# Scratch writes of row-maximum reductions sent to two bfloat16 SBUF tiles, and one output buffer instead of two, in a four-layer attention and MLP kernel

## The chip, the cores and the metric

The kernel runs on one core of one Trainium2 chip. The metric is the device time of one execution in microseconds (us); the median of three runs of the kernel before is 1586.9 us (1585.45 to 1589.74). Engines are named as in the profile: PE (matrix multiply), PEld (its weight loads), DVE (vector), ACT (scalar), POOL (GpSimd), SP (the engine that only issues DMAs here). PSUM is the memory that PE writes its products to, SBUF the working memory.

## What is computed

Two kinds of layer, A and B, follow each other twice on a sequence of 2048 rows of 640 numbers. A is attention with 32 heads of 20 dimensions, in which a row sees itself and the 255 rows before it; B is an MLP of width 1536 with a squared ReLU.

```python
def _A_ref(x, wqkv, wo):
    ...
    scores = jnp.einsum("bhqd,bhkd->bhqk", q, k) * (Dh ** -0.5)
    mask = (idx[:, None] - idx[None, :] >= 0) & (idx[:, None] - idx[None, :] < W)
    scores = jnp.where(mask[None, None], scores, -1e9)
    p = _softmax(scores, axis=-1)
    o = jnp.einsum("bhqk,bhkd->bhqd", p, v)
    return (lambda x, *d: x.transpose(*d))(o, 0, 2, 1, 3).reshape(B, S, D) @ wo
...
x = x + _A_ref(_layernorm(x, axis=-1), A_wqkv, A_wo)
x = x + _B_ref(_layernorm(x, axis=-1), B_w1, B_b1, B_w2, B_b2)
x = x + _A_ref(_layernorm(x, axis=-1), A_wqkv, A_wo)
x = x + _B_ref(_layernorm(x, axis=-1), B_w1, B_b1, B_w2, B_b2)
```

## The kernel before

**Units and quads.** The sequence is cut into 8 blocks of 256 rows; with two passes through A and B that makes 16 units, numbered 0 to 15. In a unit the 32 heads are taken four at a time: 8 quads a unit, 128 in all. Weights and activations are split into a high and a low float16 part, so each dense product is three matmuls per piece of 128 (`mm3`, L327), 256 or 320 columns wide. The dense work of a unit is: query and key rows (`stage_qk`, in the profile `acc<-yT,wq_s`), value rows (`stage_v`, `acc<-wq_s,yT`), the product with wo (`stage_o`, `acc<-wo_s,od`), and the two MLP products (`stage_f`, `acc<-y,w_s` and `acc<-w_s,hh`). In the first units some of these operands lie in borrowed tiles, so that `acc<-kt,wq_s` and `acc<-wq_s,kt` are also query, key and value work, of unit 1.

**One quad.** It has three parts on PE.
- `max_quad` (L653, L668 in the first unit of a pass) computes the raw scores into six PSUM banks, `bb6` (three for each half of the heads). DVE then makes eight reductions, `reduce` (L633): each reads 320 columns of scores from PSUM and a bfloat16 mask from SBUF (`maskq`; 128 or 256 columns and `maskw` in units 0 and 8), adds the two, writes the sum back over the scores and leaves the row maximum in `mx`. On the chip that is two instructions, the reduction and a read of the accumulator. After each two quads (a group) the maxima are turned and written into spare rows of the queries by SP DMAs (`rows_out`, L689, `qt<-mT` or `qt<-mt`): in units 0 and 1 through a PE transpose (`max_out`, L721), later through a transposing DMA (`max_cross`, L709).
- `exp_quad` (L757, L765) computes the scores again, transposed and with the maximum already subtracted, into the same six banks. ACT takes the exponentials (L779, six a quad, four in units 0 and 8) into `pt` tiles, and POOL zeroes what the window leaves out (L794, L798).
- `pv_quad` (L828) multiplies by the values. ACT copies the product to `ot` (L840), one tile for two quads, and after the second SP writes the tile to memory with four DMAs (L845). When the eight quads of a unit are written, `load_o` reads the sums and products back (L871, L872), DVE and ACT divide and split them (L904 to L914), and `stage_o` can start.

So the banks pass around a ring: scores, reductions, transposed scores, exponentials, next scores. The maxima run three quads ahead of the exponentials (`LEAD`).

**What sets the order.** The program fixes the order of every engine itself (`manual_schedule`). A planner runs while the program is built: `post` enters a job with an engine, a cost in ns, what it depends on and a priority; `pump` puts a job into the program when the planner's clock reaches it; `flow` (unit 0) and `together` (the others) ask, before each part of a quad, whether the jobs it needs are over on the planner's clock, and put pieces of dense work on PE until they are. The planned cost of a job thus sets how much dense work stands between two parts of a quad. A wait that the planner doesn't know, such as a buffer that is not yet free, is added by the framework as a semaphore wait and moves nothing. The wait of the copy into `ot` is of that kind: the planner lets `ot<-pv` depend on the product alone.

The functions that the change touches:

## Time and profile before

| | |
|---|---|
| median of three runs | 1586.9 us |
| the profiled execution | 1589.08 us, its span 1587.4 us |
| busy over the span | PE 98%, PEld 74%, DVE 62%, ACT 46%, POOL 38% |
| granted TensorE clock | 0.997 |
| costliest DVE group | the reductions L633, 409.3 us in 896 of 320 columns |
| DMA | 160.44 MB, mean 101 GB/s |

A row of a timeline gives start, duration, engine, source line, operation, output<-input, shape and count; what stands in brackets is how long the engine was idle before and what released it. Matmuls overlap in the pipeline, so the mean duration of one (around 300 ns) is not its cost; the distance from start to start is. Of the other 1.7 us of the profiled execution the span shows nothing.

### The profile page before, as it was taken

What the parts mean: (1) busy time and instruction counts of PE and PEld (TensorE: products, weight loads), DVE (VectorE), ACT (ScalarE), POOL (GpSimd) and SP (SyncE); (2) the same over time, 40 slices, a digit from 0 to 9 for tenths busy, and PEclk for the clock granted to TensorE, in tenths of its full rate; (3) what the DMA queues carried; (4) which work ended last, traced back from release to release, by engine and by line L of the source; (5) the groups of instructions that cost most, each with busy time, mean ns of one, the idle gap of its engine ahead of it and who ended that gap; (6) DMA issues with size and microseconds to landing.
All of it is one profiled execution on the core that took longest, in us unless ns stands there. A gap on an engine that the chain in (4) does not pass through costs nothing. (4 is left out here: it accounts for less than half of the span.)

```text
span 1587.4 us, 52465 instructions
## 1 busy us (share of the span) xinstructions
PE 1556.4 (98%) x21534; PEld 1167.0 (74%) x21534; DVE 984.3 (62%) x3253; ACT 733.9 (46%) x1593; POOL 600.2 (38%) x1291
## 2 busy tenths in 40 slices
PE   8989999999999999999999999999999999999999
PEld 7666767777777777778777777777777777776767
DVE  8777665656756656665566656557665666756431
ACT  4555445444453444535343453544545345454612
POOL 1234434234252433525323352442535235253612
PEclk9999999999999999999999999999999999999999
DMA  9864344362533525354352534434343353431120
GB/s 265 208 181 105 77 110 87 101 128 52 121 87 106 108 61 133 70 125 86 97 132 59 119 87 116 98 88 110 71 123 83 98 117 69 107 87 58 29 67 18
DMA packets 243209, 160.44 MB, mean 101 GB/s; under 512 B 91160, under 2 KB 226712, under 8 KB 242968
## 3 DMA queue, kind: packets, MB, share of 16 engines
q1 hardware_dynamic: 236600, 147.58, 39.3%
q10 hardware_dynamic: 6368, 9.50, 2.1%
q8 instruction: 169, 2.77, 0.8%
q14 instruction: 72, 0.59, 0.1%
HBM read 84.68 MB, written 52.95 MB: 87 GB/s over the span
## 5 line engine op out<-in xcount | busy, mean ns | idle before, releaser
L779 ACT ACTIVATE pt<-bb 128x512 f32<-128x512 f32 (+1 forms) x736 | 375.9, 601 | 226.4 <-PE bb L757 203.2
L633 DVE CUSTOM_DVE_ANT_0 bb<-bb,maskq 128x320 f32<-128x320 f32 x896 | 409.3, 523 | 89.7 <-PE bb L653 76.1
L794 POOL TENSOR_SCALAR_AFFINE_SELECT pt<-pt 128x256 f32<-128x256 f32 x448 | 188.6, 423 | 564.1 <-ACT pt L779 550.9
L327 PE MATMUL acc<-y,w_s 128*128 128x256 f16 x2880 | 330.0, 274 | 2.5 <-ACT y L377 1.4
L327 PE MATMUL acc<-w_s,hh 128*128 128x320 f16 x2304 | 326.0, 299 | 0.0
L327 PEld LDWEIGHTS <-w_s 128*128 128x128 f16 x2880 | 277.3, 98 | 55.2 <-issue 17.9
L327 PEld LDWEIGHTS <-hh 128*128 128x128 f16 x2304 | 220.6, 98 | 98.1 <-issue 11.5
L327 PEld LDWEIGHTS <-wq_s 128*128 128x128 f16 x2400 | 229.5, 98 | 46.5 <-issue 13.9
L327 PE MATMUL acc<-yT,wq_s 128*128 128x256 f16 x2250 | 258.7, 273 | 2.7 <-DVE qd L510 1.3
L798 POOL TENSOR_SCALAR_AFFINE_SELECT pt<-pt 128x256 f32<-128x256 f32 x512 | 213.6, 439 | 90.5 <-ACT pt L779 88.8
L1013 DVE TENSOR_TENSOR hh<-r,hh 128x256 f16<-128x256 f32 x192 | 95.0, 517 | 211.1 <-ACT hh L1010 204.1
L828 PE MATMUL pv<-pt,vt 128*32 128x128 f32 (+1 forms) x3840 | 190.1, 331 | 1.2 <-POOL pt L798 1.2
L1007 POOL TENSOR_TENSOR r<-r 128x256 f32<-128x256 f32 x192 | 114.3, 616 | 162.1 <-ACT r L1003 159.8
L840 ACT COPY ot<-pv 128x256 f32<-128x256 f32 x128 | 47.6, 372 | 269.3 <-PE pv L828 269.3
L327 PE MATMUL acc<-wo_s,od 128*128 128x320 f16 x960 | 140.4, 302 | 5.0 <-ACT od L911 3.0
L633 DVE DVE_READ_ACCUMULATOR2_ANT mx<- 128x1 f32 x1024 | 142.7, 139 | 0.0
L828 PEld LDWEIGHTS pv<-pt,vt 128*32 128x32 f32 x3840 | 105.2, 110 | 41.5 <-POOL pt L798 7.2
L327 PE MATMUL acc<-wq_s,yT 128*128 128x320 f16 x900 | 131.8, 299 | 1.0 <-DVE y L378 0.5
L327 PEld LDWEIGHTS <-od 128*128 128x128 f16 x960 | 91.6, 98 | 50.2 <-issue 6.4
L1003 ACT ACTIVATE r<-acc,b1s 128x256 f32<-128x256 f32 x192 | 80.5, 471 | 89.4 <-PE acc L327 88.1
L327 PEld LDWEIGHTS <-yT 128*128 128x128 f16 x900 | 85.7, 98 | 38.9 <-issue 6.3
L364 POOL TENSOR_TENSOR bmv<-bmv,neghalf 128x1 f32<-128x1 f32 x64 | 44.9, 708 | 137.4 <-DVE bmv L358 136.9
(95 smaller groups left out, 1224.4 us busy)
## 6 DMA issues: line engine op xcount, KB each, us to landing
qt<-qk SPq DMA_DIRECT2D x30, 480.0 KB
kt<-qk SPq DMA_DIRECT2D x30, 480.0 KB
qk<-qd SPq DMA_DIRECT2D x17, 640.0 KB
o<-ot SPq DMA_DIRECT2D x256, 42.0 KB
od<-o SPq DMA_DIRECT2D x14, 640.0 KB
qk<-yl SPq DMA_DIRECT2D x13, 640.0 KB
qk<-qd SPq DMA_DIRECT2D x17, 320.0 KB
xt<-in_A_x_dram SPq DMA_DIRECT2D x16, 320.0 KB
```

What stands on the lines that cost most here:

```text
L327: nc.tensor.matmul(acc, lhs(a, c), rhs(b, c), start=(k == 0), stop=(k == 3 * nk - 1))
L364: j = post("G", 520, lambda: nc.gpsimd.tensor_tensor(box["mv"][:, 3:4], box["mv"][:, 2:3], neghalf, op=ALU.pow), j, prio=prio)
L633: nc.vector.tensor_tensor_reduce(out=v, in0=v, in1=mask, scale=1.0, scalar=-3.0e38, op0=ALU.add, op1=ALU.max, accum_out=accum[e, w]),
L779: nc.scalar.activation(box["pt"][:, :o], bb[e][:, k, :o], AF.Exp, scale=SCALE / (QS * QS))
L794: nc.gpsimd.affine_select(out=m, in_=m, pattern=[[0, 2], [-1, P]], compare_op=ALU.is_gt, fill=0.0, base=0, channel_multiplier=1)
L798: nc.gpsimd.affine_select(out=m, in_=m, pattern=[[0, 2], [1, P]], compare_op=ALU.is_ge, fill=0.0, base=0, channel_multiplier=-1)
L828: nc.tensor.matmul(pv[32 * jj:32 * (jj + 1), q0 * P:(q0 + qn) * P], vf[:, c:c + 32], pj[:, j, :], start=(k == 0), stop=(k == len(steps) - ...
L840: nc.scalar.copy(ot[:, qd % 2], pv)
L1003: nc.scalar.activation(box["r"], acc[:, f, :], AF.Relu, bias=b1s[:, f0 + f:f0 + f + 1], scale=1.0 / (YS * WS))
L1007: nc.gpsimd.tensor_tensor(box["r"], box["r"], box["r"], op=ALU.mult)
L1013: nc.vector.tensor_sub(hh[:, 1, f, :], box["r"], hh[:, 0, f, :])
```

## The change

Two parts. The reductions write their sums, which nobody reads, no longer to PSUM but to one of two new tiles of 320 bfloat16 columns in SBUF, taken in turn; what is reduced and where the maximum goes stays. The planner's cost of a reduction becomes 76 + 1.047 ns a column instead of 113 + 1.047, which is 411 instead of 448 ns for 320 columns. And `ot` has one buffer instead of two.

```diff
+    junk = [sb.tile([P, 5 * Q], BF16, name=f"junk{i}") for i in range(2)]
+    junked = []
     bb6 = [ps.tile([P, 3, 512], F32, name=f"bb{e}") for e in range(2)]
...
         def reduce(e, w, v, mask, cols):
-            bbjobs.append(post("D", 113 + 1.047 * cols, lambda:
-                               nc.vector.tensor_tensor_reduce(out=v, in0=v, in1=mask, scale=1.0, scalar=-3.0e38,
-                                                              op0=ALU.add, op1=ALU.max, accum_out=accum[e, w]),
-                               prio=urgency["turn"]))
+            def put():
+                j = junk[len(junked) % 2]
+                junked.append(0)
+                nc.vector.tensor_tensor_reduce(out=j[:, :cols], in0=v, in1=mask, scale=1.0, scalar=-3.0e38,
+                                               op0=ALU.add, op1=ALU.max, accum_out=accum[e, w])
+
+            bbjobs.append(post("D", 76 + 1.047 * cols, put, prio=urgency["turn"]))
...
-            ots[u] = sb.tile([P, 2, T], F32, name="ot", bufs=2)
+            ots[u] = sb.tile([P, 2, T], F32, name="ot", bufs=1)
```

Because the cost changes, the planner's clock runs differently, and the order of the engines with it. On PE the order moves in units 0 and 1, by four matmuls in unit 2, by eight in unit 8, and from the second quad of unit 14 on; elsewhere it stays. On SP, in most units, the third of four transposing DMAs for the rows of the unit after next (L447) goes ahead of a transposing DMA of maxima (L709) instead of behind it. Line numbers below from the changed kernel are up to five higher.

The first place is PE at the start of unit 1, where the ninth quad ends (`pv`) and the tenth quad's transposed scores (L757, now L762) come. Before, the product with wo stands between them:

```order
L653 MATMUL bb_134<-kt_86,qt 64x192
L828 MATMUL pv<-pt,vt_89 32x256 x4
L828 MATMUL pv<-pt,vt_88 32x128 x4
L828 MATMUL pv<-pt,vt_91 32x128 x4
L828 MATMUL pv<-pt,vt_90 32x256 x4
L327 LDWEIGHTS od
L327 MATMUL acc<-wo_s,od 128x320
```

Of the changed kernel the same place, and behind it the end of the tenth quad's transposed scores, which the next raw scores (L658) follow after one small transpose (L726):

```order
L658 MATMUL bb_136<-kt_86,qt 64x192
L833 MATMUL pv<-pt,vt_89 32x256 x4
L833 MATMUL pv<-pt,vt_88 32x128 x4
L833 MATMUL pv<-pt,vt_91 32x128 x4
L833 MATMUL pv<-pt,vt_90 32x256 x4
L762 LDWEIGHTS kt_85
L762 MATMUL bb_135<-qt,kt_85 64x192
```

```order
L762 MATMUL bb_136<-qt,kt_86 64x192
L726 MATMUL tr<-ident,mx 16x128
L658 LDWEIGHTS qt
L658 MATMUL bb_135<-kt_85,qt 64x256
L658 LDWEIGHTS qt
```

Thirty wo matmuls stood before the tenth quad's transposed scores and thirty behind them; now all sixty come after its `pv`, and nothing dense stands between `pv`, transposed scores, raw scores and `pv`.

The second place is PE in unit 15, third quad, where the transposed scores end. Before, 22 wo matmuls follow:

```order
L757 MATMUL bb_134<-qt,kt_85 64x192
L327 LDWEIGHTS od
L327 MATMUL acc<-wo_s,od 128x320
L327 LDWEIGHTS od
L327 MATMUL acc<-wo_s,od 128x320
```

Of the changed kernel, raw scores follow at once:

```order
L762 MATMUL bb_136<-qt,kt_85 64x192
L658 LDWEIGHTS qt
L658 MATMUL bb_135<-kt_87,qt 64x256
L658 LDWEIGHTS qt
L658 MATMUL bb_136<-kt_87,qt 64x256
```

The 22 have moved behind the next `pv`. The third place is SP in unit 0: writes of `ot` (`o<-ot`), writes of the maxima (`qt<-mT`), and the query and key rows of unit 1 (`qk`, `kt`). Before:

```order
L689 DMA qt<-mT 1x8x128 x4
L542 DMA qk_0_763<-qd 128x5x512
L544 DMA qk_0_763<-qd 128x5x256
L689 DMA qt<-mT 1x8x128 x4
L845 DMA o_723<-ot 21x2x256 x4
L548 DMA qt<-qk_0_763 60x16x256 x2
L542 DMA qk_1_973<-qd 128x5x512
L544 DMA qk_1_973<-qd 128x5x256
L689 DMA qt<-mT 1x8x128 x4
L548 DMA kt_86<-qk_1_973 60x16x256 x2
L845 DMA o_723<-ot 21x2x256 x4
```

Of the changed kernel:

```order
L694 DMA qt<-mT 1x8x128 x8
L542 DMA qk_0_790<-qd 128x5x512
L544 DMA qk_0_790<-qd 128x5x256
L850 DMA o_726<-ot 21x2x256 x4
L548 DMA qt<-qk_0_790 60x16x256 x2
L694 DMA qt<-mT 1x8x128 x4
L850 DMA o_726<-ot 21x2x256 x4
L542 DMA qk_1_1037<-qd 128x5x512
L544 DMA qk_1_1037<-qd 128x5x256
L548 DMA kt_86<-qk_1_1037 60x16x256 x2
```

The second group's maxima go ahead of unit 1's query rows, and the second write of `ot` no longer stands behind the key rows. The copies into `ot` now wait for the write of the pair of quads just before, not of the pair before that.

Elsewhere dense work changes its place by some matmuls of 256 (109 ns on the planner's clock) or 320 columns (136 ns). In the tables below "cover" is the dense work that stands on PE between two parts of a quad.

| place | cover before | cover now |
|---|---|---|
| unit 0, L721 of the second group to the transposed scores of quad 2 | 10 and 40 matmuls of 256 columns, a quad's raw scores and `pv` | 10 and 25, the same |
| unit 0, transposed scores of quad 3 to the next raw scores | 11 of 320 | 5 of 256 |
| unit 0, raw scores to transposed scores of quad 1 | `pv`, 25 of 256 | `pv`, 15 of 256 |
| unit 0, last `pv` to the first wo matmul | 45 of 256, one quad's transposed scores, raw scores and `pv` | 10 of 256, 30 of 320, two quads' |
| unit 1, last quad's transposed scores to the next raw scores | 16 of 320 | 24 of 320 |
| unit 14, transposed scores of quad 2 to the next raw scores | 11 of 320 | 26 of 320 |
| unit 15, transposed scores of quad 6 to its `pv` | 40 of 256 | 35 of 256 |
| unit 15, last `pv` to the first wo matmul | 84 of 320 | 108 of 320 |

## Prediction before the run

> **What bounds the kernel now.** The busy time by stage comes first, since an average over the span mixes three regimes. The columns are the stretch, its length, and the busy time of PE, PEld, DVE, ACT and POOL with instruction counts, then the granted clock, the DMA share and GB/s.

> ```profile
> 0.00:240.00 240.00, 220.42 (x2789) 162.95 (x2790) 177.80 (x584) 120.72 (x250) 75.26 (x159) 0.99 0.61 157
> 240.00:1360.00 1120.00, 1119.98 (x15917) 843.86 (x15916) 690.75 (x2306) 520.42 (x1134) 439.57 (x958) 1.00 0.42 98
> 1360.00:1587.40 227.40, 216.03 (x2833) 160.19 (x2830) 115.78 (x364) 92.79 (x210) 85.35 (x174) 0.99 0.23 59
> ```

> From 240 to 1360 us PE lacks 0.02 us of 1120: nothing that DVE gains there can shorten anything, and the order on PE there is nearly the old one. DVE is busy for 690.75 of these 1120 us, so it follows PE and does not lead it. Only the first 240 us, where PE lacks 19.6 us, and the last 227, where it lacks 11.4, have waits to win or lose. The next view is what the change aims at, the groups of L633:

> ```profile
> L633 DVE CUSTOM_DVE_ANT_0 bb<-bb,maskq 128x320 f32<-128x320 f32 x896 | 409.3, 523 | 89.7 <-PE bb L653 76.1
> L633 DVE DVE_READ_ACCUMULATOR2_ANT mx<- 128x1 f32 x1024 | 142.7, 139 | 0.0
> ```

> The means overlap, so the cost of one is read from start to start in the DVE timeline:

> ```profile
> 610.96 0.48 DVE L633 CUSTOM_DVE_ANT_0 bb<-bb,maskq 128x320 f32<-128x320 f32 x1
> ...
> 611.37 0.53 DVE L633 CUSTOM_DVE_ANT_0 bb<-bb,maskq 128x320 f32<-128x320 f32 x1
> ...
> 611.81 0.53 DVE L633 CUSTOM_DVE_ANT_0 bb<-bb,maskq 128x320 f32<-128x320 f32 x1
> ...
> 614.51 0.48 DVE L939 SCALAR_TENSOR_TENSOR x<-acc,x 128x320 f32<-128x320 f32 x1
> 614.91 0.87 DVE L353 BATCH_NORM_STATS2 bst<-x 128x6 f32<-128x320 f32 x2
> ```

> The first reduction holds DVE for 0.41 us, the second for 0.44, since it begins beside the accumulator read of the first. L939 takes the same 320 columns from PSUM, a second input from SBUF, writes to SBUF and holds DVE for 0.40.

> **The change part by part.**

> *The reductions.* No row shows a reduction into SBUF. The nearest, L939, would save 0.01 us on each against 0.41. The bounds are -0.05 us (the accumulator read hidden altogether) and +0.05 (no reason excludes a dearer write); the 0.037 that the planner now counts on lies inside. I take -0.01, that is 0.1 us in a run of eight and 10 us of DVE time over 1024, all of it beside busy PE in the middle stage: 0 us there. The alternation adds no wait that can hurt: each reduction waits at most for the one two places before it on the same engine, which is over when its turn comes. [...]

> *One buffer of `ot`.* The copy of a pair's first quad now waits for the write of the pair just before. Rows of SP and ACT, the worst place and a common one, and the last write of all with the first reader of what it wrote:

> ```profile
> 77.64 2.08 SPq L845 DMA_DIRECT2D o<-ot  x4
> ```
> ```profile
> 82.16 0.37 ACT L840 COPY ot<-pv 128x256 f32<-128x256 f32 x1 [0.37 <-PE pv L828]
> ```
> ```profile
> 612.77 1.69 SPq L845 DMA_DIRECT2D o<-ot  x4
> ```
> ```profile
> 624.23 0.37 ACT L840 COPY ot<-pv 128x256 f32<-128x256 f32 x1 [0.65 <-PE pv L828]
> ```
> ```profile
> 1514.38 1.35 SPq L845 DMA_DIRECT2D o<-ot  x4
> 1517.14 0.58 SPq L871 DMA_DIRECT2D rs<-o  x1
> ```

> The reader starts 1.4 us after the last of the four issues, so an undisturbed write has landed by then. In the steady part the next copy comes 9.8 us after the last issue: 0 us. At 82.16 it comes 2.4 us after, which a write among the opening loads may miss by some us; ACT would stand, with weight conversions and the next exponentials queued behind the copy. But that write was late because SP held it behind the key rows of unit 1, and in the new order it isn't. I take 0; the ends are 0 and +2.4 us, another such gap.

> *The moved order, first 240 us.* The rows of PE around the second group of unit 0, and SP's:

> ```profile
> 53.58 0.72 PE L765 MATMUL bb<-qt,kt 62*128 62x256 f16 x8
> 54.23 0.28 PE L721 MATMUL tr<-ident,mx 128*16 128x128 f32 x1
> ...
> 55.80 0.67 PE L668 MATMUL bb<-kt,qt 60*128 60x128 f16 x8
> ...
> 57.19 4.54 PE L327 MATMUL acc<-kt,wq_s 128*128 128x256 f16 x40
> 61.66 0.50 PE L765 MATMUL bb<-qt,kt 62*128 62x256 f16 x8
> ```
> ```profile
> 55.66 3.79 SPq L689 DMA_DIRECT2D qt<-mT  x4
> ```

> From L721 to the scores that need its maxima pass 7.4 us, filled by 50 matmuls of 0.11 us and one quad's parts. Fifteen matmuls less leave 1.6 us open; the maxima's DMAs, now ahead of two others on SP, may go 0.5 us sooner: **+1.1** (0 to 1.6). Quad 3's raw scores get 5 matmuls of cover, 0.55 us, instead of eleven wider ones; 53.58 to 55.80, 2.2 us, is what four exponentials need, and scores, transpose and cover fill 1.1 of it: **+1.1** (0 to 1.5). Quad 1's scores lose ten matmuls in front: **+0.7** (0 to 1.1). Against that, a wait of quad 4 for its maxima goes, since they leave earlier, with matmuls that no longer compete for banks behind it:

> ```profile
> 78.61 0.49 PE L765 MATMUL bb<-qt,kt 62*128 62x256 f16 x7 [0.59 <-DMA qt<-mT]
> ```

> **-1.1** (-0.6 to -1.6; 0.59 is shown, the rest is my estimate). Then the start of unit 1:

> ```profile
> 102.87 1.41 PE L828 MATMUL pv<-pt,vt 128*32 128x256 f32 x16
> ...
> 113.45 0.33 PE L653 MATMUL bb<-kt,qt 60*64 60x256 f16 x1 [1.94 <-ACT pt L779]
> ...
> 115.15 2.36 PE L828 MATMUL pv<-pt,vt 128*32 128x256 f32 x32
> 119.81 0.45 PE L327 MATMUL acc<-wo_s,od 128*128 128x320 f16 x2 [2.31 <-ACT od L911]
> 120.53 5.55 PE L327 MATMUL acc<-wo_s,od 128*128 128x320 f16 x28 [0.27 <-DVE od L914]
> ```

> wo waits 2.6 us, and its next 28 matmuls take 5.55 us where 0.14 each would make 3.9: 4.2 us lost to operands that come 16.9 us after unit 0's last `pv`. Now 11.6 us of work (40 matmuls, two quads' parts) and their waits stand between, so wo finds its operands: **-4.2**. In its place come two waits. The tenth quad's scores follow `pv` directly: eight reductions of 0.44 us need 3.5 us, the first begins 0.9 us after its scores, and 2.8 us pass on PE: **+1.6** (1.2 to 2.4). Raw scores then follow directly; what that costs is read at a place near the end:

> ```profile
> 1376.13 0.75 PE L757 MATMUL bb<-qt,kt 62*64 62x192 f16 x32
> ...
> 1379.58 0.27 PE L653 MATMUL bb<-kt,qt 60*64 60x256 f16 x1 [1.10 <-ACT pt L779]
> ...
> 1380.07 0.75 PE L653 MATMUL bb<-kt,qt 60*64 60x256 f16 x37 [0.22 <-ACT pt L779]
> ```

> Six exponentials let raw scores run 3.9 us after the scores before them; with 0.8 us of cover **+3.1** (2.8 to 3.3). At the end of unit 1 eight more matmuls of cover take away both waits of

> ```profile
> 201.37 0.27 PE L653 MATMUL bb<-kt,qt 60*64 60x256 f16 x1 [0.42 <-ACT pt L779]
> 201.85 0.75 PE L653 MATMUL bb<-kt,qt 60*64 60x256 f16 x37 [0.22 <-ACT pt L779]
> ```

> which start to start are **-1.1**. Sum of the first 240 us: 1.1 + 1.1 + 0.7 - 1.1 - 4.2 + 1.6 + 3.1 - 1.1 = **+1.2**.

> *The moved order, from 1360 us.* At 1379.58, 26 matmuls of cover instead of 11 fill the 3.9 us: **-1.7**. In unit 15 the 22 are gone from the same interval: **+3.2**. The last rows:

> ```profile
> 1507.80 0.63 PE L828 MATMUL pv<-pt,vt 128*32 128x256 f32 x6 [1.18 <-POOL pt L798]
> ...
> 1512.41 1.51 PE L828 MATMUL pv<-pt,vt 128*32 128x256 f32 x32
> ...
> 1526.82 3.43 PE L327 MATMUL acc<-wo_s,od 128*128 128x320 f16 x24 [1.11 <-DVE od L914]
> ```

> The `pv` at 1507.80 already waits for masks; five matmuls of cover less, here and in the last quad MLP evictions on ACT and POOL beside it: **+0.8** (0 to 2). The last wo operands come 14.4 us after the last `pv`; 24 more matmuls, 3.3 us, stand between: **-1.2**. Sum: -1.7 + 3.2 + 0.8 - 1.2 = **+1.1**.

> Together +2.3 us on the profiled execution of 1589.08 us (span 1587.4 and 1.7 around it), which stood 2.2 us above the median of three. Against the median of 1586.9: **1589 us**.

> **The rivals.**
> - *Slower: unit 0's chain grows and wo still waits.* Unit 0's last `pv` now has 35 query matmuls more in front. If the operands of wo take over 11.6 + 7.7 = 19.3 us from that `pv` (7.7 are the waits at 113.45 and 115.15, 3.0, and the two new ones), wo waits again; 16.9 us are measured, so 2.4 us more decide it, a late landing of the sums among the weight loads, say. All of the 4.2 us back, and quads 1 to 3 at their dear ends: +2.3 + 4.2 + 1.3 = +7.8, 1595 us. For it: this chain passes SP, memory, DVE and ACT, the busiest stretch of each. Against: DVE's weight conversions there end earlier.
> - *Faster: unit 0 runs at its own pace anyway.* If the waits of quads 1 to 3 are only moved, since tight quads start the next ones earlier, their +2.9 fall away; with reductions 0.037 us shorter the new wait behind `pv` shrinks by 0.3 at four places, and the last quads' `pv` cost nothing: 2.3 - 2.9 - 1.2 - 0.8 = -2.6. With unit 1 starting some 3 us sooner for the same reason, -6: 1581 us. Against: the quads of unit 0 wait for DMAs, which a tighter order doesn't hurry.
> - *The reductions do not get shorter*, so the change doesn't do what the cost says, and the planner's order is 0.3 us too tight for each run of eight, felt at the four places where cover ran out: +1.2, 1590 us.
> - *ACT stands at `ot`.* Each late write costs up to 2.4 us; two at the start give +5, 1594 us. Only the opening has gaps that small.

> **How the numbers follow.** My forecast, with the third rival beside it, gets 0.50; the slower rival 0.22, `ot` 0.06, the faster one 0.22. The bounds of the terms reach from about -4 to +5 around the sum, and the rivals to 1581 and 1595; orders that differ by ten waits of 1 us leave room beyond, so the range is 1580 to 1598. A measurement here tells 0.3%, 4.8 us, from no change: faster than 1582.1 has 0.20 (most of the faster rival), slower than 1591.7 has 0.32 (both slower rivals and some of the forecast's upper end), the rest is 0.48.

> **What would show it.** The middle stage keeps 1120 of 1120 us on PE, with DVE busy less if reductions are shorter; their distance from start to start against 0.44 decides that term. The wait of wo on `od` near 120 us is gone, and raw scores wait some 3 us for ACT there and in unit 15. No `ot<-pv` waits for a DMA. The forecast is wrong if PE's gaps in the middle stage grow, if ACT waits at L845, or if the first raw scores of unit 2 move by over 4 us against 211.

## The result and the profile after

Slower, by less than 1% but clear of the noise. The changed kernel takes 1599.1 us (median of 6, 1597.2 to 1603.2) against 1589.0 of before (median of 6). The ratio on record is 1.0077, 95% interval 1.0065 to 1.0090, which is 12 us; the two medians alone are 10.1 us apart, so the loss is 10 to 12 us. The profiled execution took 1603.2 us (span 1601.5), 14.2 us more than that of before. It is the slowest of the six, with the lowest granted clock (0.989 against 0.991 to 0.993), so its trace shows more loss than the median has.

The stages first, with the columns of the prediction: stretch, length, busy time of PE, PEld, DVE, ACT and POOL, granted clock, DMA share, GB/s.

```profile
0.00:240.00 240.00, 216.17 (x2626) 158.24 (x2627) 166.09 (x565) 115.31 (x240) 68.85 (x149) 0.95 0.59 155
240.00:1360.00 1120.00, 1119.46 (x15908) 843.15 (x15907) 661.71 (x2308) 521.75 (x1136) 440.08 (x960) 1.00 0.42 97
1360.00:1601.50 241.50, 230.16 (x3004) 170.34 (x3002) 115.87 (x382) 97.21 (x217) 88.48 (x182) 0.98 0.22 60
```

The middle stage is what it was: PE is busy for 1119.46 of 1120 us, and the 29 us that DVE saves there (690.75 before) buy nothing. The loss lies in the first 240 us. PE does 163 matmuls less in them; its idle time grows from 19.6 to 23.8 us only, and the rest stands in the column of the granted clock: 0.95, where before had 0.99. Raw scores of the same quad start some 11 us later from 235 us on and 11.5 us later at 1360 us; the last stage adds 2.6.

The reductions did what the new price says. Their two groups (busy us, mean ns of one; behind the bar's second part the idle time before them), and three of a run of eight in the timeline:

```profile
L637 DVE CUSTOM_DVE_ANT_0 junk<-bb,maskq 128x320 bf16<-128x320 f32 x896 | 380.9, 484 | 102.2 <-PE bb L658 91.5 <-issue 9.8
L637 DVE DVE_READ_ACCUMULATOR2_ANT mx<- 128x1 f32 x1024 | 83.5, 82 | 0.0
```
```profile
106.61 0.49 DVE L637 CUSTOM_DVE_ANT_0 junk<-bb,maskq 128x320 bf16<-128x320 f32 x1 [1.80 <-PE bb L658]
...
107.03 0.49 DVE L637 CUSTOM_DVE_ANT_0 junk<-bb,maskq 128x320 bf16<-128x320 f32 x1
...
107.44 0.48 DVE L637 CUSTOM_DVE_ANT_0 junk<-bb,maskq 128x320 bf16<-128x320 f32 x1
```

They follow each other at 0.41 us instead of 0.45; the accumulator read fell from 139 to 82 ns.

What PE waits for in unit 0, with the rows of PE, ACT and SP:

```profile
59.31 0.50 PE L770 MATMUL bb<-qt,kt 62*128 62x256 f16 x8
...
65.27 0.76 PE L673 MATMUL bb<-kt,qt 60*128 60x128 f16 x8 [3.16 <-ACT pt L784]
```
```profile
60.02 0.58 ACT L784 ACTIVATE pt<-bb 128x512 f32<-128x512 f32 x1
63.86 0.60 ACT L507 ACTIVATE qd<-acc 128x512 f16<-128x512 f32 x1 [3.25 <-DMA qk<-qd]
64.11 0.40 ACTq L297 DMA_DIRECT2D w_s<-in_B_w_dram  x1
64.35 1.15 ACT L784 ACTIVATE pt<-bb 128x512 f32<-128x512 f32 x3
```
```profile
54.62 2.74 SPq L694 DMA_DIRECT2D qt<-mT  x4
57.46 0.39 SPq L542 DMA_DIRECT2D qk<-qd  x1
57.90 0.52 SPq L544 DMA_DIRECT2D qk<-qd  x1
```

The raw scores of quad 5 wait 3.16 us for quad 2's exponentials. ACT has taken one of them and then stands 3.25 us at the eviction of a key product: the one buffer of `qd` still holds unit 1's queries, whose two writes to memory now leave SP at 57.46 and 57.90, behind the four issues of maxima rows. Before, they left at 54.59 and 55.02, ahead of the rows, and the eviction at 59.59 waited for nothing.

Then the start of unit 1:

```profile
121.37 1.12 PE L327 MATMUL acc<-wq_s,yT 128*128 128x320 f16 x7
125.11 1.77 PE L658 MATMUL bb<-kt,qt 60*64 60x256 f16 x38 [2.61 <-ACT pt L784]
126.81 2.24 PE L833 MATMUL pv<-pt,vt 128*32 128x256 f32 x32
130.05 0.24 PE L762 MATMUL bb<-qt,kt 62*64 62x192 f16 x1 [1.01 <-DVE mx L637]
130.47 0.75 PE L762 MATMUL bb<-qt,kt 62*64 62x192 f16 x31 [0.17 <-DVE mx L637]
131.15 0.28 PE L726 MATMUL tr<-ident,mx 128*16 128x128 f32 x1
134.25 1.76 PE L658 MATMUL bb<-kt,qt 60*64 60x256 f16 x38 [2.83 <-ACT pt L784]
135.95 2.78 PE L833 MATMUL pv<-pt,vt 128*32 128x256 f32 x32
138.66 8.32 PE L327 MATMUL acc<-wo_s,od 128*128 128x320 f16 x60
```

The waits at 130.05 and 134.25 were forecast, and that of wo is gone. But look at the durations: the raw scores of a quad take 1.77 us here, 37 of their 38 matmuls took 0.75 before at 201.85; 32 of `pv` take 2.78, not 1.51. The granted clock says why; four stretches of it, three of the changed kernel and one of before:

```profile
65.40:70.40 5.00, 4.94 (x39) 2.80 (x37) 3.68 (x18) 2.35 (x5) 1.32 (x3) 0.66 1.06 254
131.70:138.60 6.90, 4.23 (x70) 2.49 (x69) 5.58 (x14) 4.32 (x10) 4.02 (x8) 0.51 0.72 148
1473.20:1480.10 6.90, 6.15 (x78) 3.56 (x78) 3.85 (x14) 1.77 (x5) 2.61 (x7) 0.51 0.01 2
```
```profile
120.30:123.80 3.50, 3.27 (x13) 1.90 (x14) 3.50 (x15) 0.46 (x1) 0.00 (x0) 0.51 1.16 217
```

### The profile page after: what moved, and what is told of

Its sections match the earlier page's. It is cut to its first block, busy times and chain, and to the rows that moved or that the text cites. A ratio compares the mean times of both kernels' runs of the same rounds, so it can differ in the third digit from the quotient of the medians.

```text
span 1601.5 us, 52593 instructions
## 1 busy us (share of the span) xinstructions
PE 1565.8 (98%) x21534; PEld 1171.7 (73%) x21534; DVE 943.7 (59%) x3253; ACT 734.3 (46%) x1593; POOL 597.4 (37%) x1291
## 5 line engine op out<-in xcount | busy, mean ns | idle before, releaser
L637 DVE CUSTOM_DVE_ANT_0 junk<-bb,maskq 128x320 bf16<-128x320 f32 x896 | 380.9, 484 | 102.2 <-PE bb L658 91.5
L327 PE MATMUL acc<-y,w_s 128*128 128x256 f16 x2880 | 331.7, 274 | 4.4 <-DVE y L378 2.5
L327 PE MATMUL acc<-w_s,hh 128*128 128x320 f16 x2304 | 326.1, 299 | 0.0
L327 PEld LDWEIGHTS <-w_s 128*128 128x128 f16 x2880 | 278.2, 98 | 58.0 <-issue 20.2
L327 PEld LDWEIGHTS <-hh 128*128 128x128 f16 x2304 | 220.7, 98 | 98.3 <-issue 11.9
L327 PEld LDWEIGHTS <-wq_s 128*128 128x128 f16 x2400 | 230.1, 98 | 46.9 <-issue 13.5
L327 PE MATMUL acc<-yT,wq_s 128*128 128x256 f16 x2250 | 259.3, 273 | 1.1 <-DVE wq_s L260 0.6
L833 PE MATMUL pv<-pt,vt 128*32 128x128 f32 (+1 forms) x3840 | 193.7, 334 | 2.2 <-POOL pt L803 2.2
L845 ACT COPY ot<-pv 128x256 f32<-128x256 f32 x128 | 47.7, 373 | 277.5 <-PE pv L833 233.3
L327 PE MATMUL acc<-wo_s,od 128*128 128x320 f16 x960 | 139.0, 301 | 0.0
L327 PE MATMUL acc<-wq_s,yT 128*128 128x320 f16 x900 | 133.7, 302 | 0.5 <-DVE kt L378 0.5
L327 PEld LDWEIGHTS <-od 128*128 128x128 f16 x960 | 91.6, 98 | 44.4 <-issue 7.4
L327 PEld LDWEIGHTS <-yT 128*128 128x128 f16 x900 | 86.2, 98 | 39.3 <-issue 5.3
L658 PE MATMUL bb<-kt,qt 60*64 60x64 f16 (+3 forms) x4256 | 88.4, 225 | 8.6 <-ACT pt L784 8.1
```

What stands on the lines that cost most here:

```text
L327: nc.tensor.matmul(acc, lhs(a, c), rhs(b, c), start=(k == 0), stop=(k == 3 * nk - 1))
L637: nc.vector.tensor_tensor_reduce(out=j[:, :cols], in0=v, in1=mask, scale=1.0, scalar=-3.0e38, op0=ALU.add, op1=ALU.max, accum_out=accum[e, w])
L658: nc.tensor.matmul(flat[e][rows, o:o + b - a], qt[r, p, i * P + 64 * h:i * P + 64 * (h + 1)], kt[r, p, a + to:b + to], start=True, stop=Tr ...
L833: nc.tensor.matmul(pv[32 * jj:32 * (jj + 1), q0 * P:(q0 + qn) * P], vf[:, c:c + 32], pj[:, j, :], start=(k == 0), stop=(k == len(steps) - ...
L845: nc.scalar.copy(ot[:, qd % 2], pv)
```

## The experiments

Quads are numbered through the units: 0 to 7 are unit 0, 8 to 15 unit 1. Theory at the start: the planner's new price moves the order, and the order costs everything, by waits and by the half-speed stretches that follow them. Rivals: the write to SBUF or the single `ot` costs by itself; or the waits cost and the clock doesn't.

| run | order | ratio | 95% interval |
|---|---|---|---|
| e1 | of before | 1.0000 | 0.9988 to 1.0013 |
| e4 | of before | 1.0006 | 0.9995 to 1.0017 |
| e2 | of the changed kernel | 1.0091 | 1.0073 to 1.0108 |
| e9 | changed in units 0 to 7 | 1.0070 | 1.0058 to 1.0083 |
| e10 | changed in units 14, 15 | 1.0009 | 1.0000 to 1.0017 |
| e15 | new price in unit 0 only | 1.0064 | 1.0047 to 1.0080 |
| e16 | new price in unit 1 only | 1.0045 | 1.0029 to 1.0062 |
| e12, price 60 | a third | 1.0065 | 1.0052 to 1.0078 |
| e13, price 95 | a fourth | 1.0069 | 1.0054 to 1.0084 |
| e6 | changed, two writes earlier | 1.0070 | 1.0057 to 1.0083 |
| e5, e7, e14, fills | changed | 1.0059, 1.0053, 1.0053 | e14: 1.0035 to 1.0072 |
| e8, fills | of before | 1.0026 | 1.0016 to 1.0036 |

### Which part of the change

e1: the changed kernel with the old price.

```diff
-            bbjobs.append(post("D", 76 + 1.047 * cols, put, prio=urgency["turn"]))
+            bbjobs.append(post("D", 113 + 1.047 * cols, put, prio=urgency["turn"]))
```

> The changed kernel with the planner's old price of a reduction, 113 + 1.047 ns per column: it still writes to the two SBUF tiles and still has one buffer of ot, and every engine issues its instructions in the order of before. Theory (the moved order costs everything): 1588 us, ratio 0.998 to 1.001 of before, reductions 0.41 us apart, three stretches of granted clock 0.5, as before. Rival (the write to SBUF or the single ot costs time by itself): ratio 1.004 to 1.008.

e2: before with the new price alone.

```diff
-            bbjobs.append(post("D", 113 + 1.047 * cols, lambda:
+            bbjobs.append(post("D", 76 + 1.047 * cols, lambda:
```

> The kernel before with only the planner's price lowered to 76 + 1.047 ns per column: PSUM writes and two ot buffers stay, every engine issues in the order of the changed kernel. Theory (the moved order costs everything): ratio 1.006 to 1.010, some 1599 us, with six or more stretches of granted clock 0.5 in the first 240 us; the reductions, 0.45 us apart again, may add 1 to 2 us where eight of them stand on the path. Rival (SBUF write or ot): ratio 0.998 to 1.002.

e4: before with one buffer of `ot`.

```diff
-            ots[u] = sb.tile([P, 2, T], F32, name="ot", bufs=2)
+            ots[u] = sb.tile([P, 2, T], F32, name="ot", bufs=1)
```

> The kernel before with one buffer of ot instead of two and nothing else; the issue order is that of before on every engine. Theory: no copy waits for a write for long outside the opening, ratio 0.999 to 1.002; at the second pair of unit 0 the copy may wait up to 2.4 us for its write. Rival (ACT stands at ot): ratio 1.003 or more, with waits of ot<-pv for a DMA.

Measured: e1 1587.9 us, ratio 1.0000; e2 1602.1 us, 1.0091; e4 1588.5 us, 1.0006. The reductions' groups in e1 and in e2:

```profile
L637 DVE CUSTOM_DVE_ANT_0 junk<-bb,maskq 128x320 bf16<-128x320 f32 x896 | 380.7, 484 | 90.0 <-PE bb L658 75.9 <-issue 11.7 <-ACT pt L784 1.7
L637 DVE DVE_READ_ACCUMULATOR2_ANT mx<- 128x1 f32 x1024 | 83.4, 81 | 0.0
```
```profile
L633 DVE CUSTOM_DVE_ANT_0 bb<-bb,maskq 128x320 f32<-128x320 f32 x896 | 409.5, 523 | 102.3 <-PE bb L653 88.4 <-issue 13.2
L633 DVE DVE_READ_ACCUMULATOR2_ANT mx<- 128x1 f32 x1024 | 143.1, 140 | 0.0
```

e1 has the cheaper reductions and gains nothing; e2 has the dear ones and loses as much as the change. So the order is the cause, and the cheaper write is worth nothing here that twelve runs can tell (within 0.13%, 2 us). In e4, ACT does once stand long at the one buffer:

```profile
83.23 0.37 ACT L840 COPY ot<-pv 128x256 f32<-128x256 f32 x1 [3.52 <-DMA o<-ot]
```

That is the place that the prediction named (82.16 in before). PE loses 1.1 us to it, at L721, and the ratio stays 1.0006. In the changed order no copy comes more than 0.5 us after its product and ACT's work ahead of it.

### Where, and at what price

e9 and e10: the new price in units 0 to 7 only, and from unit 8 on only.

```diff
-            bbjobs.append(post("D", 76 + 1.047 * cols, put, prio=urgency["turn"]))
+            bbjobs.append(post("D", (76 if u < 8 else 113) + 1.047 * cols, put, prio=urgency["turn"]))
```

> The changed kernel with the planner's new price of a reduction in units 0 to 7 and the old one from unit 8 on: every engine has the order of the changed kernel up to there and that of before behind it. Theory by the trace (first 240 us +11, last 230 us +3 of 14 us): most of the loss stays, 9 to 11 us, ratio 1.0055 to 1.0075. Rival (the end costs most): ratio 1.001 to 1.004.

> The reverse of the split run: the old price in units 0 to 7, the new one from unit 8 on, so the order of before up to there and that of the changed kernel in units 14 and 15; writes to SBUF and one ot throughout. Theory (the first units hold the loss; the end has as much idle time in both orders, 11.4 against 11.3 us): ratio 0.999 to 1.002. Rival (the end costs 3 us of its own): 1.002 to 1.004.

Measured: 1.0070 and 1.0009. The loss is in the first units. Of the 2.6 us that the last stage took in the profiled execution half is left in the runs: e10 has the same 2.70 us wait in unit 15 and comes out 1.4 us above before.

e15 and e16: `76 if u == 0` and `76 if u == 1` in the same line.

> The changed kernel with the new price of a reduction for the raw scores of unit 0 alone and the old price from unit 1 on: every engine has the order of the changed kernel up to the last quads of unit 0, and from there a third order. Theory (unit 0's tight order starts the loss: ACT stands behind the query writes, and the products it pulled ahead are missing in unit 1): ratio 1.005 to 1.009. Rival (unit 1's order is the dear one): 1.000 to 1.003.

> The changed kernel with the new price for the raw scores of unit 1 alone and the old one elsewhere: the order of before in unit 0, on all engines, and little moved behind it (596 of 37179 places on PE, four DMA issues on SP). Theory (the loss starts in unit 0): ratio 0.999 to 1.003. Rival (unit 1's order is the dear one): 1.004 to 1.009.

Measured: 1.0064 and 1.0045. The theory held for unit 0 and fell for unit 1: an order that differs from that of before in 596 of 37179 places on PE costs 7 us. Its rows of PE and DVE show a wait that before doesn't have:

```profile
125.84 0.75 PE L762 MATMUL bb<-qt,kt 62*64 62x192 f16 x31 [0.17 <-DVE mx L637]
128.94 0.28 PE L726 MATMUL tr<-ident,mx 128*16 128x128 f32 x1 [2.35 <-DVE x L944]
```
```profile
128.39 0.89 DVE L944 SCALAR_TENSOR_TENSOR x<-acc,x 128x320 f32<-128x320 f32 x2 [2.52 <-DMA x<-in_A_x_dram]
```

PE wants the bank of a wo product, DVE cannot empty it, since the input rows that it adds come late from SP's queue. The two losses don't add (e15 and e16 together would be 1.011, both units give 1.0070): each order has its own waits.

e12 and e13: the price 60 and 95 instead of 76.

> The changed kernel with a price of 60 instead of 76 ns plus 1.047 per column, 0.395 us for a reduction that takes 0.41: one more order of units 0, 1, 14 and 15, from a price too low. Theory (any price re-deals the waits at both ends, and the nearest to the truth is not the best): somewhere between 0.997 and 1.012, not ranked by the price's error. Rival (a shorter price makes the order tighter and so worse): 1.009 or more.

> The changed kernel with a price of 95 ns plus 1.047 per column, 0.43 us for a reduction, between the true 0.41 and the old 0.448. Theory (any price re-deals the waits): between 0.997 and 1.012. Rival (the time grows steadily as the price falls from 113 to 76): 1.003 to 1.005.

Measured: 1599.2 us, 1.0065, and 1598.3 us, 1.0069. Not ranked by the price's error: 76 + 1.047 per column gives 0.411 us, just what a reduction takes now, and does no better than 60 or 95; 113, 9% too high, is the best of the four.

### Can the wait at 65 us be moved away

e6: the rows' four issues on SP behind the two query writes, as before.

```diff
-        def spread():
+        def spread(hold=hold):
+            if hold:
+                held_rows.append(lambda: spread(False))
+                return
...
             nc.sync.dma_start(drv[:, c0:c0 + n, 2 - 2 * j, :], qd[:, c0:c0 + n, 0, :])
+            while (u, j) == (1, 0) and held_rows:
+                held_rows.pop()()
```

> The changed kernel with four DMA issues moved on SP: the maxima rows of quads 2 and 3 of unit 0 are issued behind the two writes of unit 1's queries instead of ahead of them, as before the change; no other instruction moves on any engine. Theory (ACT stands 3.2 us at the eviction of the next product because the query writes that free its tile leave 2.9 us later on SP, and the raw scores of quad 5 wait for the exponentials behind it): that wait goes, with it most of the 3.2 us of PE at 65 us and the half-speed stretch behind it (1.7 us); the rows come up to 1 us later. Ratio 1.004 to 1.0065. Rival (the write is late because the DMA queues are full, wherever it is issued): the wait stays, ratio 1.007 to 1.009.

Measured: 1598.7 us, 1.0070. SP and PE of this run:

```profile
55.01 0.39 SPq L542 DMA_DIRECT2D qk<-qd  x1
55.44 0.53 SPq L544 DMA_DIRECT2D qk<-qd  x1
56.01 3.69 SPq L701 DMA_DIRECT2D qt<-mT  x4
```
```profile
60.77 1.16 PE L777 MATMUL bb<-qt,kt 62*128 62x256 f16 x8 [2.60 <-DMA qt<-mT]
```

The cause of the wait was right: ACT no longer stands, and the 3.16 us at quad 5 are gone. The time stays in the rival's range even so, since in their place quad 2's scores wait 2.60 us for their maxima rows. Two sets of issues share SP, and one of them is late, whichever goes first. That the 15 matmuls less on PE between L721 and quad 2's scores are the reason is likely but not shown: no run puts them back. The half-speed stretch stays as well.

### What the clock costs

e5: idle matmuls ahead of the raw scores that wait, written to the product bank that nobody reads any more; 18 each for quads 11, 12 and 125.

```diff
+        for _ in range(FILL.get(n, 0)):
+            t = recent[-2]
+            nc.tensor.matmul(t[:, 0, :P] if len(t.shape) > 2 else t[:, :P], ident, ident, start=True, stop=True)
```

> The changed kernel with 18 idle matmuls of 0.11 us (identity by identity, written to the product bank that nobody reads any more) put on PE ahead of the raw scores of quads 11, 12 and 125, where PE waits 2.6, 2.8 and 2.7 us for ACT; they fill 2.0 us of each wait and nothing else moves. Theory (a wait costs its own length and, where a stretch of 3.4 us holds too little PE work, a half-speed stretch of 3.4 us behind it): the stretches of clock 0.5 near 125, 132 to 138 and 1473 to 1480 us go, 1.6 + 2.1 + 3.0 = 6.7 us less than the changed kernel, 1592 to 1594 us, ratio 1.002 to 1.005. Rival (only the waits themselves cost): 1599 us as before the fill, ratio 1.007, or dearer.

Measured: 1597.1 us, ratio 1.0059 (1.0042 to 1.0076). The size was wrong: one such call is two matmuls (36 in the trace for 18 calls) and takes 0.22 us, so the fills ran past the waits. e7 has 10 each, e14 nine each and six ahead of quad 9's scores.

> As the run with 18 idle matmuls ahead of the raw scores of quads 11, 12 and 125, but with 10: one of them takes 0.22 us and not 0.11, so that 18 took 4.2 to 5.7 us and ran 1.3 to 2.9 us past the end of each wait; 10 take 2.2 us and stay inside. Theory (waits bring half-speed stretches of 3.4 us): the stretches at 125, 132 to 138 and 1473 to 1480 us stay away at no cost, 6 to 7 us less than the changed kernel, ratio 1.002 to 1.005. Rival (only the waits themselves cost): as the changed kernel, ratio 1.007 to 1.009.

> The changed kernel with idle matmuls of 0.22 us in four waits of PE instead of three, sized to stay inside: 9 ahead of the raw scores of quads 11, 12 and 125 and 6 ahead of the scores of quad 9, whose wait of 1.0 to 1.7 us had brought a half-speed stretch in the run with 10, which then made the fill of quad 12 overrun by 1 us. Theory (about 0.6 us of run time for each us of clock lost in these stages, as the runs of one kernel scatter): only the stretches near 36 and 77 us stay, 3.4 us of lost clock, ratio 1.003 to 1.0045. Rival (the stretches cost little, since the next wait takes back what a faster clock wins): 1.005 to 1.007.

Measured: 1596.2 us, 1.0053 (1.0039 to 1.0066), and 1596.1 us, 1.0053. The first stage of e14:

```profile
0.00:240.00 240.00, 220.64 (x2744) 164.92 (x2745) 169.88 (x575) 117.88 (x246) 71.36 (x155) 0.99 0.60 156
```

The clock is back at 0.99, and over six executions at 0.9965 on average, against 0.9970 of before and 0.9912 of the changed kernel. The ratio falls from 1.0077 to 1.0053 and no further, 3 to 4 us. e7 lies between its two expectations; e14 lies in the range of its rival, with an interval that reaches into both. The stretches cost, but less than half of the loss by this measure.

e8: fills in the order of before, with seven calls ahead of quad 11's raw scores and nine behind the last `pv` before `stage_o`.

> The changed kernel with the old price, so in the order of before, with idle matmuls of 0.22 us in its two longest waits of PE: 7 ahead of the raw scores of quad 11 (1.9 us of wait near 113 us) and 9 behind the last product of probabilities and values before stage_o of unit 0 (2.3 us of wait near 120 us). Theory (waits bring half-speed stretches): the two stretches near 114 and 121 us, 1.6 to 1.7 us each, stay away: ratio 0.997 to 0.999, 1584 to 1586 us, faster than both kernels. Rival (only the waits cost): ratio 0.9995 to 1.001.

Measured: 1592.0 us, 1.0026, slower, against both expectations. Both stretches did go. PE's next wait took it all:

```profile
124.01 0.91 PE L771 MATMUL bb<-qt,kt 62*64 62x192 f16 x32
127.06 0.28 PE L735 MATMUL tr<-ident,mx 128*16 128x128 f32 x1 [2.14 <-DVE x L955]
```
```profile
126.52 0.89 DVE L955 SCALAR_TENSOR_TENSOR x<-acc,x 128x320 f32<-128x320 f32 x2 [2.39 <-DMA x<-in_A_x_dram]
```

It is the wait for the input rows again: in before the half-speed matmuls ran while those rows were on their way (DVE waited 0.78 us for them, at 125.57), and cost little there. Why the run is 4 us slower, and not equal, is only partly seen. In the profiled execution the same quads start only 0.2 us later than in before at 244 us, and 2.4 of its 2.9 us come with a wait of 1.99 us in unit 14 that before lacks, far from the fills. Why it is there, and whether the other executions have it, no trace shows.

e11 prices a stretch where nothing else is late: idle copies on ACT in 20 quads of units 3 to 12, in the kernel before.

```diff
                 def power(k=k, e=e, o=o, box=box):
+                    for _ in range(DOSE.get(n, 0) if (k, e) == (1, 0) else 0):
+                        nc.scalar.copy(idle, maskw[:, :192])
```

> The kernel before with idle copies on ACT (128x192 bfloat16, SBUF to SBUF, results unused) ahead of the third exponential of two quads in each of units 3 to 12: 6, 8, 10, 12 or 14 of them, four quads each, 200 in all; no order moves. They make PE wait in the stretch where it otherwise never does, so that waits of several lengths can be read against the granted clock. Theory (PE's clock is halved for a stretch of 3.41 us when the stretch of 3.41 us ahead of it held too little PE work): waits of 1 us leave the clock alone, waits of some 2 us and more bring a stretch or not by how they fall on the grid, those of 3 us nearly always; each stretch adds 1.7 us to its unit, since nothing else is waited for here. Time over before = sum of the waits + 1.7 us times the number of stretches, within 3 us. Rival (a half-speed stretch costs less, 0.6 of that, or nothing): the sum of the waits and at most 1 us per stretch.

Measured: 1644.2 us, ratio 1.0350 (1.0335 to 1.0365). Pairs of stretches ahead of and behind a wait of 2.11, of 1.51 and of 3.04 us:

```profile
484.60:488.00 3.40, 1.42 (x11) 0.89 (x9) 0.54 (x3) 3.24 (x10) 0.78 (x3) 1.00 0.00 0
488.90:492.20 3.30, 3.30 (x65) 1.93 (x54) 2.15 (x7) 1.41 (x2) 1.73 (x4) 0.50 0.02 5
536.00:539.40 3.40, 2.01 (x19) 1.66 (x17) 0.97 (x4) 3.24 (x10) 0.83 (x3) 1.00 0.00 0
539.50:542.90 3.40, 3.11 (x75) 2.02 (x75) 1.85 (x4) 1.44 (x3) 2.36 (x5) 1.00 0.53 43
741.40:744.80 3.40, 0.90 (x9) 0.67 (x7) 0.00 (x0) 3.21 (x10) 0.41 (x2) 1.00 0.00 0
744.80:751.60 6.80, 6.13 (x79) 3.82 (x79) 3.66 (x9) 3.25 (x7) 2.88 (x6) 0.50 0.56 74
```

The nine waits of 0.57 to 1.67 us all left the clock at 1.00. Those of 2.11 (two), 2.28 (two) and 2.87 us each brought one stretch of 3.41 us, those of 3.04 us (two) two in a row: nine in all. Six waits of 0.73 to 1.05 us that followed in the same or the next quad left it at 1.00 too. From the same quads of before to those of e11, the stage is 60.0 us longer; from start to start of PE's matmuls 46.1 us of it are waits at full clock, and 13.9 fall in the nine stretches, 1.5 us each of the 1.7 that half clock takes from 3.41. That is the theory; where PE alone is the bound, as in these units of e11, a stretch costs nearly what it slows. PE was not idle ahead of them: by the rows it was busy for 1.42 of the 3.40 us from 484.60 on, and for 0.90 of those from 741.40 on.

The length of one wait does not decide, though. The changed kernel has a stretch at 155.66 us behind two waits of 1.10 and 0.94 us, and e6 has none behind the 2.70 us of unit 15. The first row is of the changed kernel, the others are of e6:

```profile
152.24:155.65 3.41, 1.37 (x11) 0.94 (x10) 2.46 (x5) 3.27 (x8) 1.02 (x3) 1.00 0.31 101
1466.97:1470.38 3.41, 2.04 (x42) 1.34 (x41) 3.37 (x11) 1.28 (x3) 0.53 (x2) 1.00 0.12 34
1470.38:1473.80 3.42, 1.87 (x66) 1.41 (x69) 1.40 (x5) 2.10 (x5) 3.23 (x8) 1.00 0.01 2
```

In one execution the stretches start whole multiples of 3.41 us apart (in the changed kernel at 36.19, 66.91 and 80.56), and on that grid e6's wait is cut in two. In the traces of all these kernels, cut by their grids from 20 us on, PE was busy for 7 to 62% of the piece ahead of a stretch that follows full clock, and for 44% or more of every piece that none follows.

The executions of one kernel give a second price. Over 66 of before, taken beside the experiments, whose granted clock ran from 0.993 to 0.999, the span rises by 0.72 us (0.52 to 0.89) for each us of clock lost (1 minus the clock, times the span): 1584.7 us at 0.999, 1586.1 at 0.997, 1588.0 at 0.995, 1593.2 at 0.993. This is a correlation, in which the clock goes with half of the variance, and it holds the waits that bring the stretches too. The changed kernel loses 9.3 us more of the clock, 6.7 us at that price; the fills say 3 to 4. Of the 10 to 12 us, then, an estimated 3 to 7 are the clock and the rest longer waits; a closer split stays open.

## Why the prediction was wrong

The sign of the sum was right, the size was not: +2.3 us forecast, 10 to 12 measured, and 1599.1 us is 1 us above the range. The sign was in part luck, since most waits forecast for unit 0 did not come and others did.

- **Middle stage, reductions and `ot`:** right. The reduction's saving was mis-sized, 0.01 us by L939 against 0.038 measured (0.449 to 0.411 us from start to start, inside the bounds): L939 was set against the first reduction of a run, 0.41, and those behind it took 0.45. The saving buys nothing in e1. A dearer write, which the bound of +0.05 us allowed for, no run shows: from start to end, too, a reduction takes 0.48 us against 0.52 before. `ot` cost 0 as taken.
- **The end:** right in three waits and near in the sum, +1.1 forecast and 1.4 in e10. The wait at 1379.58 went (-1.7), that in unit 15 came (2.70 at 1473.82, forecast 3.2), wo's wait at 1526.82 went. But the idle time of the last stage did not grow (11.3 us against 11.4 before); what grew in the profiled execution is PE work lost at half clock, 4.7 us against 1.7.
- **Unit 1's start:** the waits were right. wo's wait went, quad 9's scores wait 1.2 us (forecast 1.6), the raw scores behind them 2.83 (forecast 3.1), those at 201 us are gone. The -4.2 came too: the sixty wo matmuls from 138.66 on take 0.14 us each. But I had misread what it was made of, the 5.55 us of wo's next 28 matmuls as operands that came late. The row of before above, 0.51 between 120.30 and 123.80, shows half clock: 1.6 of the 4.2 us were the price of the wait ahead. The waits that came in its place paid that price as well, 6.8 us at half clock from 131.76 on, and the sum has no term for it.
- **Unit 0, the step that failed:** "the maxima's DMAs, now ahead of two others on SP, may go 0.5 us sooner: +1.1". The rows did go sooner, and quad 2's scores wait for nothing, nor do quad 1's (forecast +0.7). The two others were the writes that free `qd`, and what they hold up was not asked: ACT stands 3.25 us, PE 3.16. A queue was priced for what moves forward in it and not for what is moved back. Up to unit 0's last `pv` (102.87 us before, 115.49 now) PE idles 3.8 us more in the profiled executions, where the terms of unit 0 add up to +1.8, and loses 5.0 us more to half clock, for which they have nothing; the rest of the 12.6 us is the work of the 35 query matmuls that now stand ahead of it. e6 shows that exchanging the issues back is no cure: that order has its own 2.60 us.
- **What the sum lacked:** any term for the clock. PE's idle time in the first 245 us grew by 4.8 us in the profiled executions, where +1.2 was forecast, and PE work lost at half speed there grew by another 7.1 us. The row of the first stage stood in the prediction with its 0.99, and nothing was made of it. The last of the signs of being wrong that the prediction named did come: the raw scores of 211 us start 11.8 us later.
- **The rivals:** the slower one named the wrong mechanism (wo does not wait again), though its 1595 us were nearest. The faster one argued that tight quads start the next ones earlier; they start the next wait earlier. "The reductions do not get shorter" is false.

## What to carry to other kernels

A planner's price that is nearer the truth is not a better order: measure the order by itself (old order with the new operation, new order with the old one) before crediting or blaming the operation. A kernel bound by PE can pay twice for a PE wait, once for the wait and once for a half-speed stretch behind it (in e11 46.1 us and 13.9 us). In these traces such a stretch followed full clock only where PE had stood for 38% or more of the 3.41 us piece ahead (1.3 us), and always where it had stood for more than 56% (1.9 us), so waits that fall close together can cost more than apart: 1.10 and 0.94 us in one piece brought a stretch in the changed kernel, nine of 0.57 to 1.67 us in e11 brought none; the column of the granted clock by stage shows it. When issues trade places on a queue, follow the one that was pushed back to the buffer that it frees.

## What the hardware showed that I had not expected

- The half clock comes with PE far from idle: in the changed kernel PE was busy for 2.13 of the 3.41 us ahead of the stretch at 36.19. In e11 seven waits of 2.11 to 3.04 us brought it each time and nine of 0.57 to 1.67 us never; elsewhere two of 1.10 and 0.94 us in one piece of the grid brought it, and one of 2.70 us that the grid cuts in two did not. It lasts 3.41 us or a multiple, 6.83 us at 131.76 in the changed kernel and up to four times that near 123 us in e2 and e9 (13.65 us).
- About half of the variance of this kernel's executions (1584.8 to 1594.9 us) goes with it. In the same order on PE the traces have three stretches (before, e1) or one (e4).
- A reduction with accumulator that writes to SBUF instead of PSUM gains more on the accumulator read (139 to 82 ns) than on itself (523 to 484 ns). The two overlap, and from start to start a reduction gains 38 ns. The sums are also bfloat16 now instead of float32; no run tells that apart.
